# A seven-product step that adds one product onto ScalarE's copy in PSUM, and joins one pair more

## The chip, the cores and the metric

The kernel runs on one core of one Trainium2 chip. A core has TensorE (matrix products, PE in the profile, with its weight loads as PEld), VectorE (DVE), ScalarE (ACT), GpSimd (POOL) and SyncE (SP, which issues DMAs here). Each engine works through its own queue in order; engines wait for each other through semaphores. The metric is the time of one execution on the device in microseconds (us).

## The reference

```python
for t in range(S):                       # attention block: B, H, S, D = 4, 8, 768, 48
    cur = einsum('bhd,bhe->bhde', u * k[t], v[t])
    y[t] = einsum('bhd,bhde->bhe', r[t], state + cur)
    state = w[t][..., None] * state + einsum('bhd,bhe->bhde', k[t], v[t])
x = y.transpose(0, 2, 1, 3).reshape(B * S, H * D)      # 3072 tokens x 384
h = x @ w_in                                           # 384 -> 2048
g = h - tanh(h)
return g @ w_out                                       # 2048 -> 384
```

All arrays are float32. This case is about the product `x @ w_in`.

## The kernel before

The 3072 tokens are handled in eight blocks of 384 (`NB`; a half, `HB`, is 192). While block i passes through the dense part, the attention part of block i + 1 is computed in the gaps. The order of the work on TensorE, VectorE, ScalarE and SyncE is written out by hand: what the Python code emits first is first in its engine's queue. Inside a block the loop runs over f = 0 to 15, one tile of 128 of the 2048 inner columns at a time.

**First product.** An unjoined f calls `first` (L899): three matmuls of 128x384, one for each third of the 384 inputs, accumulated in the PSUM bank `hp`. The profile shows each float32 matmul as two instructions. Two neighbouring f, a pair j = f // 2, can be *joined* instead: their 2x2 split (two column tiles by two token halves) is computed by a scheme with seven products of the kind Strassen's is, each 192 wide, from sums of weights (`s1` to `s5`, `weight_forms`) and sums of tokens (`t1` to `t4`, `token_forms`) that VectorE makes beforehand. `JOINED` names the joined pairs of each block: three in block 2, six in blocks 3 to 6 (pairs 0, 1, 2, 3, 4, 7), seven in block 7; 34 in all. `Twos.begin` (L948) emits, at the even f, the 11 matmuls of the seven products (L961, 22 instructions), a ScalarE copy of the first product into the SBUF tile `joint` (L962), and four VectorE additions (L971), three of 384 columns and one of 192. The additions come back as a list and are put between VectorE's other work by the loop.

The products land in two PSUM tiles of two banks each, `att0` and `att1` (`ps_a.both`, here e0 and e1; "att" in the profile). The attention part uses the same two tiles for its score products (L508), its state update (L589, read by VectorE at L601) and its results (L785), in turn, through `Kept.tile`.

**After the first product.** `slight` (L987 to L991) emits two tanh per f on ScalarE and a square, which ScalarE or VectorE does; `product` (L905) makes g from them on VectorE; `form_g` (L1010) makes sums of g.

**Second product.** `Fewer` does a scheme of 15 products of 128x128 per pair (L1096). Twelve of them go to the banks `acc0` to `acc2`, six per call of `add`, one call per f through `add_due`. The last three ("others") go to a bank of their own: for pairs 0 to 3 at f = 9, for pairs 4 to 7 during the next block, at f = 0 and f = 2 where its pair 0 is joined; in both cases `hp`. ScalarE copies the first half of them out (L1109), VectorE adds the second half to that (`others_summed`, L1124). The banks `acc` are copied out by ScalarE at the start of the next block (L1109).

**Attention steps in a block** (`plan`): in blocks from 3 on, score products at f = 2, preceded by ScalarE's splits (L556); joins of transposed keys on ScalarE at f = 6 to 9 (L566); state update at f = 10; results at f = 12. VectorE's products at f = 0 and 1 are L450 and L457.

`EMPTY` gives each block a number of no-ops, which `apart` puts between TensorE's matmuls.

Of the kernel before, what the change touches and what calls it, by code (L numbers as in the profile page):

```python
# [37 lines left out]
F32 = mybir.dt.float32  # L38
# [13 lines left out]
P = 128  # L52
L = 64
# [83 lines left out]
def kernel(  # L137
# [59 lines left out]
    def draw(names, cols):  # L197
        nc.gpsimd.memset(mask_all[0:L, cols], 1.0)
        for m in names:
# [5 lines left out]
            else:  # L205
# [13 lines left out]
    states = [states0[:, 0:NPAIR * NCH * L].rearrange("d (p c e) -> d p c e", c=NCH, e=L),  # L219
              const.tile([P, NPAIR, NCH, L], F32, name="states1", tag="states1")]  # L220
# [109 lines left out]
    joint = const.tile([P, 6 * HB], F32, name="joint", tag="joint")  # L330
# [3 lines left out]
    class Block:  # L334
# [258 lines left out]
        def update_2(self):  # L593
# [9 lines left out]
            if self.q > 0:  # L603
                step(St[:, :, 0, 0:D], St[:, :, 0, 0:D], tot(0), ALU.mult)
            for c in range(NCH - 1 if self.q == NQ - 1 else NCH):
                dst = St[:, :, c + 1, 0:D] if c + 1 < NCH else states[self.q + 1][:, :, 0, 0:D]
# [304 lines left out]
    class Twos:  # L911
# [15 lines left out]
        def results(self, *tiles):  # L927
            self.to = [t[:, 0:6 * HB].rearrange("p (n t) -> p n t", t=HB) for t in tiles]
# [19 lines left out]
        def begin(self, ps, j):  # L948

            h = self.to[j % len(self.to)]  # L950
            e0, e1 = ps.both[(ps.n + 1) % 2], ps.both[ps.n % 2]
# [4 lines left out]
            for to, *of in ((e0[:, 1, 0:HB], (a11, b11)), (e0[:, 0, 0:HB], (a12, b21), (a13, b31)),  # L956
                            (e0[:, 0, HB:NB], (s2, t2)), (e1[:, 0, 0:HB], (s3, t3)),
                            (e1[:, 0, HB:NB], (s1, t1), (a23, b32)), (e1[:, 1, 0:HB], (s4, b22), (s5, b32)),
                            (e1[:, 1, HB:NB], (a22, t4), (a23, b31))):
                for n, (lhs, rhs) in enumerate(of):  # L960
                    nc.tensor.matmul(to, lhsT=lhs, rhs=rhs, start=n == 0, stop=n + 1 == len(of))  # L961
            nc.scalar.copy(out=h[:, 3], in_=e0[:, 1, 0:HB])  # L962

            def both(t):
                return t.rearrange("p (n t) -> p n t", t=HB)
# [390 lines left out]
    for i, blk in enumerate(blocks):  # L1356
# [10 lines left out]
        for f in range(NF):  # L1367
# [23 lines left out]
            if joined and f == 9:  # L1391
                fewer.others(ps_a, range(4), hp)
# [225 lines left out]
```

## Time and profile before

| | us |
|---|---|
| median of 3 runs | 537.61 (536.73 to 537.94) |
| the profiled execution | 535.64 |
| its span, first to last instruction | 533.9 |
| TensorE busy (matmuls) | 523.9 (98%) |
| VectorE busy | 478.1 (90%) |
| ScalarE busy | 312.4 (59%) |
| granted TensorE clock | 0.999 |

A row of a grouped view has the line, engine, operation, tiles (out<-in), shape and count, then the busy time, the mean duration of one in ns, and the idle time of the engine just before, with what ended it. A row of the timeline has the start, the length, the engine, line and operation, how many instructions it merges, and in brackets the idle time before it and what ended it. A row of the chain of waits has start, length, engine, tile, line and count.

### The profile page before, as it was taken

What the parts mean: (1) busy time and instruction counts of PE and PEld (TensorE: products, weight loads), DVE (VectorE), ACT (ScalarE), POOL (GpSimd) and SP (SyncE); (2) the same over time, 40 slices, a digit from 0 to 9 for tenths busy, and PEclk for the clock granted to TensorE, in tenths of its full rate; (3) what the DMA queues carried; (4) which work ended last, traced back from release to release, by engine and by line L of the source; (5) the groups of instructions that cost most, each with busy time, mean ns of one, the idle gap of its engine ahead of it and who ended that gap; (6) DMA issues with size and microseconds to landing.
All of it is one profiled execution on the core that took longest, in us unless ns stands there. A gap on an engine that the chain in (4) does not pass through costs nothing.

```text
span 533.9 us, 14969 instructions
## 1 busy us (share of the span) xinstructions
PE 523.9 (98%) x6040; PEld 449.2 (84%) x6040; DVE 478.1 (90%) x1011; ACT 312.4 (59%) x729; POOL 9.1 (2%) x57
## 2 busy tenths in 40 slices
PE   7999999999999999999999999999999999999996
PEld 5756665677887879999799998999889997999994
DVE  7999996698889999999999999999999999667874
ACT  4999984665536473655646375375735655454350
POOL 1100000000000000000000000000000000000001
PEclk9999999999999999999999999999999999999999
DMA  8799632352312452035420832145321430200011
GB/s 282 258 406 342 224 120 71 107 132 64 122 26 72 104 143 95 0 89 166 120 58 2 192 119 66 54 66 142 108 88 31 79 116 1 58 1 1 10 36 48
DMA packets 53048, 56.35 MB, mean 106 GB/s; under 512 B 21488, under 2 KB 50928, under 8 KB 52976
## 3 DMA queue, kind: packets, MB, share of 16 engines
q1 hardware_dynamic: 52592, 55.18, 34.7%
q8 instruction: 49, 0.80, 0.6%
q14 instruction: 23, 0.19, 0.1%
q10 hardware_dynamic: 288, 0.10, 0.1%
q0 software_dynamic: 96, 0.07, 0.1%
HBM read 44.73 MB, written 4.72 MB: 93 GB/s over the span
## 4 chain that ended last, share of the span: by engine, by line
PE 83%; DVE 13%; issue 2%; DMA 1%; SPq 0%; DVEq 0%
PE acc L1096 23%; PE att L961 20%; PE hp L899 17%; PE acc L1047 6%; PE hp L1096 5%; PE att L785 3%; DVE g L1010 2%; PE att L508 2%; DVE joint L971 2%; DVE g L905 1%; PE att L589 1%; DVE pre L431 1%; PE acc L1074 1%; PE att L1096 1%; PE att L899 1%
## 5 line engine op out<-in xcount | busy, mean ns | idle before, releaser
L1096 PE MATMUL acc<-forms,g 128*128 128x128 f32 x972 | 135.5, 276 | 0.0
L1096 PEld LDWEIGHTS acc<-forms,g 128*128 128x128 f32 x972 | 124.3, 192 | 3.8
L899 PE MATMUL hp<-xT,w_sb 128*128 128x384 f32 x330 | 116.5, 489 | 0.0
L1010 DVE TENSOR_TENSOR g<-g 128x256 f32<-128x256 f32 x270 | 110.5, 418 | 6.1 <-DVE g L1010 0.5
L899 PEld LDWEIGHTS hp<-xT,w_sb 128*128 128x128 f32 x330 | 59.5, 190 | 33.3
L905 DVE SCALAR_TENSOR_TENSOR g<-h,qa 128x384 f32<-128x384 f32 x112 | 61.7, 551 | 18.1 <-ACT h L991 17.9
L987 ACT ACTIVATE h<-joint 128x384 f32<-128x384 f32 x54 | 27.9, 517 | 77.5 <-DVE joint L971 77.5
L961 PE MATMUL att<-xT,w_sb 128*128 128x192 f32 x340 | 72.0, 326 | 0.0
L987 ACT ACTIVATE h<-hp 128x384 f32<-128x384 f32 x55 | 27.2, 495 | 58.5 <-PE hp L899 58.4
L991 ACT ACTIVATE h<-h 128x384 f32<-128x384 f32 x113 | 58.2, 515 | 0.0
L961 PEld LDWEIGHTS att<-xT,w_sb 128*128 128x128 f32 x340 | 56.4, 190 | 0.0
L971 DVE TENSOR_TENSOR joint<-joint,att 128x384 f32<-128x384 f32 (+1 forms) x108 | 51.6, 499 | 4.9 <-PE att L961 3.0
L1096 PE MATMUL acc<-w_sb,g 128*128 128x128 f32 x324 | 54.5, 277 | 0.0
L1096 PEld LDWEIGHTS acc<-w_sb,g 128*128 128x128 f32 x324 | 45.9, 192 | 4.4
L961 PE MATMUL att<-turned,kept 128*128 128x192 f32 x192 | 36.5, 327 | 0.1
L1132 DVE TENSOR_TENSOR sums<-sums 128x256 f32<-128x256 f32 x84 | 33.3, 410 | 1.4 <-ACT sums L1109 0.9
L1047 PE MATMUL acc<-w_sb,sums 128*128 128x384 f32 x96 | 33.7, 487 | 0.0
L272 ACT ACTIVATE up<-raw 128x768 f16<-128x768 f32 (+1 forms) x32 | 33.0, 1108 | 0.0
L961 PEld LDWEIGHTS att<-turned,kept 128*128 128x128 f32 x192 | 32.0, 190 | 0.4 <-DVE turned L945 0.4
L1096 PE MATMUL hp<-w_sb,g 128*128 128x128 f32 x176 | 29.5, 275 | 0.0
L1047 PEld LDWEIGHTS acc<-w_sb,sums 128*128 128x128 f32 x96 | 18.1, 190 | 12.3
L988 ACT ACTIVATE qa<-joint 128x384 f32<-128x384 f32 x54 | 27.5, 509 | 0.0
(157 smaller groups left out, 795.5 us busy)
## 6 DMA issues: line engine op xcount, KB each, us to landing
raw<-in_weights SPq DMA_DIRECT2D x16, 768.0 KB, 7.4
w<-in_wT SPq DMA_DIRECT2D x7, 780.0 KB, 4.4
k<-in_kT SPq DMA_DIRECT2D x7, 768.0 KB, 4.6
r<-in_rT SPq DMA_DIRECT2D x7, 768.0 KB, 4.5
v_sb<-in_v SPq DMA_DIRECT2D x8, 576.0 KB, 5.1
k<-in_tokens SPq DMA_DIRECT2D x7, 576.0 KB, 4.1
r<-in_tokens SPq DMA_DIRECT2D x7, 576.0 KB, 4.2
out_y<-sums SPq DMA_DIRECT2D x18, 128.0 KB, 1.9
```

The costliest lines, as they stand in the source:

```text
L272: return lambda: nc.scalar.activation(out=to, in_=of, func=AF.Copy, scale=scale, bias=bias)
L899: nc.tensor.matmul(hp, lhsT=w_in_sb[:, f, kc, :], rhs=xT[kc], start=(kc == KC - 1), stop=(kc == 0))
L905: return lambda: nc.vector.scalar_tensor_tensor(out=out, in0=in0, scalar=scalar, in1=in1, op0=op0, op1=ALU.mult)
L961: nc.tensor.matmul(to, lhsT=lhs, rhs=rhs, start=n == 0, stop=n + 1 == len(of))
L971: return [lambda of=of: nc.vector.tensor_tensor(out=of[0], in0=of[1], in1=of[2], op=ALU.add) for of in ((h[:, 0:5:4], twice(h[:, 3]), both ...
L987: made = nc.scalar.activation(out=t, in_=h, func=AF.Tanh, scale=INNER / UPSCALE)
L988: nc.scalar.activation(out=by, in_=h, func=AF.Tanh, scale=OUTER / UPSCALE)
L991: nc.scalar.activation(out=t, in_=t, func=AF.Square, accum_out=top[:, n:n + 1])
L1010: return lambda: nc.vector.tensor_tensor(out=G[:, to:to + 2], in0=two(G, g_at(q, a0), g_at(q, a1)), in1=two(G, g_at(q, b0), g_at(q, b1)), ...
L1047: nc.tensor.matmul(acc, lhsT=g[:, j * P:(j + 1) * P], rhs=w_out_sb[:, f, :], start=(f == self.first), stop=(f == NF - 1))
L1096: nc.tensor.matmul(to, lhsT=G[:, g_at(q, a), :], rhs=rhs, start=start, stop=stop, skip_group_check=True)
L1132: ops.append(lambda op=op, at=at: nc.vector.tensor_tensor(out=at[0], in0=at[1], in1=at[2], op=OPS[op]))
```

## The change

`Twos.begin` is rearranged. The first product goes to e0's bank 1, and ScalarE copies it to the left half of the bank `hp` (before: to SBUF). s3 t3 and s1 t1 (+ its second term) go to e1's bank 0, and ScalarE copies both, 384 columns, to SBUF; (a22, t4) and its second term go to e1's bank 1; s2 t2 is accumulated by TensorE onto the copy in `hp`. Two additions of 384 columns follow on VectorE. The remaining four matmuls (two terms accumulated onto the first product, and s4, s5) are emitted by a new function `end` after those additions; they follow on TensorE's queue directly, and a third addition of 192 columns works in place in PSUM. The tanh of the pair's first half reads e0's bank 1 instead of SBUF.

`hp` is then no longer free for the others: they go to e0's bank 0, for pairs 4 to 7 all at f = 1 (where the block's pair 0 is joined) and for pairs 0 to 3 at f = 9; they are summed out right ahead of pair 1. Pair 5 is joined in blocks 2 to 6 too, which makes 39 joined pairs; the weight forms of pair 5 move from the set made late for block 7 to a set made in block 2. The order of the two `att` tiles is set anew at the score products and at the state update (`ps.n = 0`). The states lose their padding (64 to 48 columns), `joint` shrinks from six to three halves, and the no-ops are counted anew.

```diff
-BESIDE = (0, 1, 2, 3, 4, 7)
-EMPTY = (159, 0, 92, 0, 16, 0, 40, 0)
-JOINED = {2: (1, 4, 7), 3: BESIDE, 4: BESIDE, 5: BESIDE, 6: BESIDE, 7: TWOS}
-PAIRS = range(0, 1), range(1, 2), range(2, 3), range(3, 5), range(7, 8)
-LEFT = range(5, 7)
+BESIDE = (0, 1, 2, 3, 4, 5, 7)
+EMPTY = (159, 0, 72, 0, 0, 150, 10, 0)
+JOINED = {2: (1, 4, 5, 7), 3: BESIDE, 4: BESIDE, 5: BESIDE, 6: BESIDE, 7: TWOS}
+PAIRS = range(0, 1), range(1, 2), range(2, 3), range(3, 6), range(7, 8)
+LEFT = range(6, 7)
...
+            if name in ("earlier", "update"):
+                ps.n = 0
...
-            h = self.to[j % len(self.to)]
-            e0, e1 = ps.both[(ps.n + 1) % 2], ps.both[ps.n % 2]
+            to, (e0, e1) = self.to[j % len(self.to)], ps.both
...
-            for to, *of in ((e0[:, 1, 0:HB], (a11, b11)), (e0[:, 0, 0:HB], (a12, b21), (a13, b31)),
-                            (e0[:, 0, HB:NB], (s2, t2)), (e1[:, 0, 0:HB], (s3, t3)),
-                            (e1[:, 0, HB:NB], (s1, t1), (a23, b32)), (e1[:, 1, 0:HB], (s4, b22), (s5, b32)),
-                            (e1[:, 1, HB:NB], (a22, t4), (a23, b31))):
-                for n, (lhs, rhs) in enumerate(of):
-                    nc.tensor.matmul(to, lhsT=lhs, rhs=rhs, start=n == 0, stop=n + 1 == len(of))
-            nc.scalar.copy(out=h[:, 3], in_=e0[:, 1, 0:HB])
+            c11, c12 = (e0[:, 1, n * HB:(n + 1) * HB] for n in range(2))
+            sixth = hp[:, 0:HB]
+
+            def products(*groups):
+                for to, start, *of in groups:
+                    for n, (lhs, rhs) in enumerate(of):
+                        nc.tensor.matmul(to, lhsT=lhs, rhs=rhs, start=start and n == 0, stop=n + 1 == len(of),
+                                         skip_group_check=True)
...
-            return [lambda of=of: nc.vector.tensor_tensor(out=of[0], in0=of[1], in1=of[2], op=ALU.add)
-                    for of in ((h[:, 0:5:4], twice(h[:, 3]), both(e0[:, 0, 0:NB])),
-                               (h[:, 5:3:-1], twice(h[:, 4]), both(e1[:, 0, 0:NB])),
-                               (h[:, 1], h[:, 4], e1[:, 1, 0:HB]),
-                               (h[:, 2:4], twice(h[:, 5]), e1[:, 1::-1, HB:NB]))]
+            products((c11, True, (a11, b11)))
+            nc.scalar.copy(out=sixth, in_=c11)
+            products((e1[:, 0, 0:HB], True, (s3, t3)), (e1[:, 0, HB:NB], True, (s1, t1), (a23, b32)))
+            nc.scalar.copy(out=to[:, 2::-2], in_=e1[:, 0, 0:NB].rearrange("p (n t) -> p n t", t=HB))
+            products((e1[:, 1, HB:NB], True, (a22, t4), (a23, b31)), (sixth, False, (s2, t2)))
+
+            def end():
+                products((c11, False, (a12, b21), (a13, b31)), (c12, False, (s4, b22), (s5, b32)))
+                return [adding(c12, to[:, 0], c12)]
+
+            self.end = end
+            self.h = [e0[:, 1, 0:NB], to[:, 1:3].rearrange("p n t -> p (n t)")]
+            return [adding(to[:, 2::-2], to[:, 2::-2], twice(sixth)),
+                    adding(to[:, 1:3], twice(to[:, 2]), e1[:, 1::-1, HB:NB])]
...
             if joined and f == 9:
-                fewer.others(ps_a, range(4), hp)
+                fewer.others(ps_a, range(4), ps_a.both[0][:, 0])
+            if joined and f == 1 and summed:
+                summed[0].others(ps_a, (4, 5, 6, 7), ps_a.both[0][:, 0])
...
-            if f == 3 and summed and 0 in JOINED.get(i, ()):
-                spare.append(summed[0].others_summed)
...
-            elif outs and later:
-                ops = between(rest, carried) + outs[:1] + formed + outs[1:] + spare
-                carried = []
             elif outs:
-                ops = (between(rest, carried) + outs[:1] + formed + spare[:-1] + outs[1:2] + spare[-1:] + outs[2:])
-                carried = []
+                early_spare, spare = ([], spare) if later else (spare[:-1], spare[-1:])
+                run(between(rest, carried) + outs[:1] + formed + early_spare + outs[1:])
+                ops, carried = twos.end() + spare, []
             elif joined and later:
-                ops, behind = behind + between(forming, spare) + rest + formed, []
+                ops = (between(forming + rest + formed, behind) + spare if len(behind) > 2 else
+                       behind + between(forming, spare) + rest + formed)
+                behind = []
...
-                if f in (0, 2) and summed and 0 in JOINED[i]:
-                    summed[0].others(ps_a, (4,) if not f else (5, 6, 7), hp)
...
+            if joined and f == 1 and summed:
+                behind.append(summed[0].others_summed)
```

More of the change, by code (lines that the diff above doesn't have):

```diff
@@ L329 @@
     turned = const.tile([P, 2 * NB], F32, name="turned", tag="turned")
-    joint = const.tile([P, 6 * HB], F32, name="joint", tag="joint")
+    joint = const.tile([P, 3 * HB], F32, name="joint", tag="joint")
     empty = []
@@ L927, in results @@
         def results(self, *tiles):
-            self.to = [t[:, 0:6 * HB].rearrange("p (n t) -> p n t", t=HB) for t in tiles]
+            self.to = [t[:, 0:3 * HB].rearrange("p (n t) -> p n t", t=HB) for t in tiles]
         def weight_forms(self, n, which):
@@ L1324 @@
     twos = Twos()
-    for pairs, at in zip(PAIRS, (0, 1, 2, 3, 5)):
+    for pairs, at in zip(PAIRS, (0, 1, 2, 3, 6)):
         twos.form(pairs, [kept[:, (x * len(BESIDE) + at) * P:(x * len(BESIDE) + at + len(pairs)) * P]
@@ L1484 @@
             if i == 1 and f == 6:
[L1485 removed]
+                nc.gpsimd.memset(states[0][:, :, 0], 0.0)
             if not i and "update" in phases.get(f, ()):
@@ L1556 @@
             make_identity(nc, unit[0])
-            for st in states:
-                nc.vector.memset(st[:, :, :, D:], 0.0)
             for blk in [Block(b, q) for b in range(B) for q in range(NQ)]:
```

16 lines of the change are left out of this document (7 added, 9 removed).

## The prediction

> **What bounds the kernel now.** I read the page's busy shares and chain first, then a table by stage over one block of tokens, then the chain of waits by line inside that block.
>
> ```profile
> span 533.9 us, 14969 instructions
> ...
> PE 523.9 (98%) x6040; PEld 449.2 (84%) x6040; DVE 478.1 (90%) x1011; ACT 312.4 (59%) x729; POOL 9.1 (2%) x57
> ...
> PE 83%; DVE 13%; issue 2%; DMA 1%; SPq 0%; DVEq 0%
> ```
> ```profile
> 277.60:340.30 62.70, 62.70 (x767) 58.61 (x767) 60.36 (x129) 35.75 (x92) 0.32 (x4) 1.00 0.36 92
> ```
> ```profile
> 301.18 3.58 PE att L961 x22
> 304.76 2.68 PE acc L1096 x24
> ...
> 318.39 1.43 PE att L589 x80
> 319.81 1.53 PE acc L1096 x12
> 321.35 1.94 PE hp L899 x6
> 323.29 1.34 PE acc L1096 x12
> ```
>
> The second fence is block 4 (columns: window, its length, busy PE, PEld, DVE, ACT, POOL, granted clock, DMA share, GB/s). TensorE is busy for 62.70 of 62.70 us and VectorE for 60.36. So whatever makes TensorE wait inside a block is added to the time, and whatever VectorE sheds is worth only what TensorE waited for it, which here is nearly nothing. A joined pair costs TensorE 3.58 us (22 matmuls, 0.163 each); an unjoined pair costs two runs of 1.94, so 3.88; six products of the second stage cost 1.34, the 12 matmuls of one call.
>
> **What it removes and adds.** Pair 5 becomes joined in blocks 2 to 6: TensorE gains 3.88 - 3.58 = 0.30 us five times, 1.5 us. Joined pairs go from 34 to 39. Each loses one 384-wide addition and gains a 384-wide ScalarE copy out of PSUM:
>
> ```profile
> L971 DVE TENSOR_TENSOR joint<-joint,att 128x384 f32<-128x384 f32 x81 | 44.3, 547 | 4.0 <-PE att L961 3.0 <-ACT joint L962 1.0
> L971 DVE TENSOR_TENSOR joint<-joint,att 128x192 f32<-128x192 f32 x27 | 9.6, 354 | 0.9
> L757 ACT COPY xT<-att 128x384 f32<-128x384 f32 x22 | 9.2, 496 | 0.0
> L1010 DVE TENSOR_TENSOR g<-g 128x256 f32<-128x256 f32 x270 | 110.5, 418 | 6.1 <-DVE g L1010 0.5 <-PE acc L1096 0.3
> L905 DVE SCALAR_TENSOR_TENSOR g<-h,qa 128x384 f32<-128x384 f32 x112 | 61.7, 551 | 18.1 <-ACT h L991 17.9
> ```
>
> VectorE sheds 34 x 0.55 = 18.6 us and takes 5 x (2 x 0.55 + 0.35) = 7.2 us for the new pairs, so it ends about 11 us lighter; ScalarE takes 39 x 0.50 = 19 us more on 312. The addition that writes to PSUM has no row; the same size in SBUF is 0.35 and I take that. All of this lies beside TensorE's work, so I cost it at nothing on the path. The forms of pair 5's weights move between two sets whose total stays; the narrower state tiles change strides only; the no-ops are issued between matmuls of at least 0.11 us. These too I cost at nothing (0.3 us either way).
>
> **The wait that is new.** Before, no TensorE instruction inside a run of joined products waits for ScalarE. After, two do: s2 t2 adds onto ScalarE's copy in hp, and (a22, t4) writes bank 1 of tile e1 after ScalarE was told to copy bank 0 of it. Whether the second is a wait depends on how the program's waits are set, by bank or by tile. The run at 334.04 answers it for reads:
>
> ```profile
> 334.04 1.14 PE L961 MATMUL att<-xT,w_sb 128*128 128x192 f32 x6
> ...
> 335.02 1.14 PE L961 MATMUL att<-turned,kept 128*128 128x192 f32 x6
> ...
> 335.54 0.32 ACT L962 COPY joint<-att 128x192 f32<-128x192 f32 x1 [1.26 <-PE att L961]
> ...
> 338.84 0.52 ACT L987 ACTIVATE h<-joint 128x384 f32<-128x384 f32 x1 [2.98 <-DVE joint L971]
> ...
> 339.27 0.51 ACT L988 ACTIVATE qa<-joint 128x384 f32<-128x384 f32 x1
> ...
> 340.19 0.51 ACT L987 ACTIVATE h<-joint 128x384 f32<-128x384 f32 x1
> ```
>
> The copy reads the first product alone, which is two matmuls and lands at 334.04 + 0.163 + 0.33 = 334.53. ScalarE stood idle for 1.26 us and still began at 335.54. That is when the eighth matmul lands (334.04 + 7 x 0.163 + 0.33 = 335.51), the last into tile e0, in its other bank. So a read waits for the whole two-bank tile. For writes no stall in the trace isolates the question, but the program's list of waits does: the matmul that opens the results (L785) waits for the state addition (L601) that reads the other bank of its tile, though neither its own bank nor its operands need that one. I take it that the rule is the tile.
>
> Then (a22, t4) waits in every joined pair. The eighth matmul lands at 1.47 us from the start of the run, the copy begins at 1.50 (as above), takes 0.50 (L757), and TensorE starts 0.05 us behind its releaser, as here, where the merged additions end at 228.70 + 1.40 = 230.10:
>
> ```profile
> 228.70 1.40 DVE L971 TENSOR_TENSOR joint<-joint,att 128x384 f32<-128x384 f32 x3
> ...
> 230.15 0.64 PE L508 MATMUL att<-pre,post 48*64 48x64 f32 x28 [0.72 <-DVE joint L971]
> ```
>
> That is 2.05, or 2.15 with a weight load that nothing hides, where it would have issued at 8 x 0.163 = 1.30: 0.75 to 0.85 us. I take 0.80, so **39 x 0.80 = 31 us**. Bounds: 29 and 33; nothing at all if waits go by bank.
>
> **What the wait drags behind it.** After, the tanh of a pair's first half hangs on a chain through all engines: the run is 3.58 + 0.80 = 4.38 long, VectorE's last addition follows at about 4.85 to 5.20, both tanh are over at 6.2 (0.94 from 338.84 to 339.78), and ScalarE is free after two halves of 1.35 each (338.84 to 340.19), at 7.95. Against that stand, in a full block, with these rows:
>
> ```profile
> 287.34 2.94 ACT L556 COPY w<-post 128x768 uint16<-128x768 uint16 x3
> ...
> 287.94 0.95 DVE L450 TENSOR_TENSOR pre<-r,pre 128x768 f32<-128x768 f32 x1
> ...
> 290.18 1.09 ACT L1109 ACTIVATE sums<-acc 128x512 f32<-128x512 f32 x2
> ...
> 291.58 1.81 PE L508 MATMUL att<-pre,post 48*64 48x64 f32 x96
> ```
> ```profile
> 309.67 0.75 ACT L566 COPY ks<-ks 128x512 uint16<-128x512 uint16 x1
> ...
> 310.29 0.30 ACT L962 COPY joint<-att 128x192 f32<-128x192 f32 x1
> ```
> ```profile
> 317.36 2.02 ACT L566 COPY ks<-post 128x512 uint16<-128x512 uint16 x3
> ...
> 321.77 0.35 DVE L601 TENSOR_TENSOR states<-states,whole 128x192 f32<-128x192 f32 x1
> ...
> 326.51 0.36 DVE L601 TENSOR_TENSOR states<-states,whole 128x192 f32<-128x192 f32 x1
> ...
> 327.83 1.56 PE L785 MATMUL att<-pre,states 48*48 48x64 f32 x96
> ```
>
> - The fourth-column products ("others") at f = 1 and f = 9 now write tile e0, which tanh still reads: TensorE is there at 4.38 + 1.34 = 5.72 and waits to 6.25: 0.5 us, twice.
> - Pair 1's first product waits for VectorE to sum those products out of e0. VectorE, from 5.20: one product of 0.95, three of 0.95, three forms and another at 0.42, one of 0.55, and the sum of 0.55, to 11.8. TensorE, from 6.25: 24 matmuls of 0.112 (2.7) and 1.34, to 10.3. 1.5 us.
> - The second score product at f = 2 writes e0 and so waits for pair 1's tanh, behind ScalarE's three splits (2.0 + 2.94) and the two copies of 1.09 that need TensorE's 5.9: to 7.0, then 0.94. TensorE is there at 5.72 + 0.9: 1.35 us. Before, the moved products covered this.
> - Pair 4: two joins of 0.75 hold ScalarE to 9.45, and TensorE begins at 4.38 + 2.68 = 7.06; the copies of 0.32 and 0.50 end 3.2 into the run, not 2.0: 1.2 us. (At 310.29 the copy is this late already, 3.0 us into the run at 307.3, and nothing waits.)
> - Pair 5, by the same count with the 0.75 and 2.02 joins and the copy of the others' half: 1.5 us.
> - The results (L785) wait for the states: VectorE takes 5.1 us (321.77 to 326.87), TensorE's cover shrinks from 8.0 us (319.82 to 327.83) to 1.34 + 1.94 + 1.34 = 4.6, and VectorE starts behind pair 5's additions: 1.5 us.
>
> That is 8.05 us in each of blocks 3 to 6, some 3.5 in block 2 (the others at f = 9, pair 5, the results) and 1.0 in block 7 (the others twice): 37 us. Each stands on a queue position that I derived and shrinks when VectorE, 0.55 us lighter per pair, is ahead; I take six tenths, 22 us. Ends: -1 (none, and the small stall at 230.15 gone) and 44.
>
> **Sum.** Against the profiled execution's 535.64 us (1.7 us around its span; the median of the runs is 2.0 above it): 535.6 - 1.5 + 31 + 22 = 587, so **589 us** as a median; I say 590.
>
> **Rivals.**
> 1. *Waits go by bank*, and only the read's wait was late. For it: the change keeps each engine in a bank of its own. Against it: the copy at 335.54, held by the other bank. Without the 31 us, the score product (1.35), the results (1.5) and pair 4 keep their waits; pair 4's is then s2 t2 behind the copy in hp: ScalarE is free at 9.45 - 0.80 = 8.65, the run begins at 3.58 + 2.68 = 6.26, so the copy ends 2.7 into it and is needed at 12 x 0.163 = 1.96: 0.75 us. That is 3.6 x 4 + 2.2 (block 2) - 1.5 = 15: 553 us. The Trainium skill states the rule that this rival needs, in "PSUM — Partial Sum Buffer", "Summary: rules for kernel authors": a read beside running matmuls should aim at another bank, and semaphores guard by bank; by it nothing would have to wait at the ninth matmul, and the trace of before shows this program waiting for more than that.
> 2. *Faster.* By bank, and VectorE, lighter by 0.55 per pair, brings tanh so far forward that no copy is late: TensorE keeps the 1.5 us and the stall of 0.72 at 230.15, and the time is about 535.5. It decides from where ScalarE is free 1.2 us into each run. For it: ScalarE is 59% busy. Against it: 310.29.
> 3. *The change gives nothing.* The 1.5 us is lost again to one or two waits per block: 537.6.
>
> **How the numbers follow.** The forecast, waits by tile, 0.86; rival 1, 0.04; rival 2, 0.07; rival 3, 0.03. The forecast's own range runs from 537.6 + 29 - 1.5 - 1 = 564 to 537.6 + 33 + 44 - 1.5 = 613; I give **560 to 616**, which leaves out the rivals and a little more. A measurement of this kernel tells about 0.2% (1.1 us) from nothing. Faster 0.07, within 0.2% 0.03, slower 0.90.
>
> **What would show it.** In the profile after, the run of 22 matmuls should be cut in two or three pieces, with TensorE idle about 0.8 us in front of the ninth matmul, released by the copy of the two products, 39 times; the waits view should hold a row of TensorE on that copy of some 30 us and more. TensorE's busy share should fall to about 90%, and VectorE's busy time to about 467 us. The forecast falls if the ninth matmul follows the eighth after 0.16 us; then rivals 1 and 2 are parted by the score product at f = 2 and the results. The second sum falls if the ninth waits and the grams, the others and L785 do not: then it is about 567.

## The result: 595.4 us after, 537.5 before

| | before | after |
|---|---|---|
| median of the runs | 537.49 (536.73 to 537.94) | 595.35 (594.42 to 597.78) |
| profiled execution | 535.64 | 594.77 |
| its span | 533.9 | 593.0 |

The ratio is 1.1085, 95% interval 1.1048 to 1.1122: slower by 58 us. The forecast was 590, range 560 to 616.

From the page of the changed kernel, its span, busy times and the chain by engine:

```profile
span 593.0 us, 15237 instructions
...
PE 538.7 (91%) x6090; PEld 457.2 (77%) x6090; DVE 469.5 (79%) x992; ACT 329.5 (56%) x773; POOL 9.1 (2%) x57
...
PE 62%; DVE 17%; ACT 13%; issue 4%; DMA 2%; SPq 1%; PEld 0%; PEldq 0%; DVEq 0%; ACTq 0%
```

TensorE was 98% busy and is 91% busy; on the chain its share falls from 83% to 62%, and ScalarE, which was not on it, has 13%. VectorE ended 8.6 us lighter (478.1 to 469.5) and ScalarE 17.1 heavier, as the change intends. None of that is the 58 us. It is TensorE's waits, here by what it waited for (us in total, times, longest):

```profile
PE att L965 <- ACT joint L977: 27.7, 32, 1.8
PE att L508 <- ACT qa L1000: 4.3, 4, 1.1
PE att L1108 <- ACT qa L1000: 3.4, 5, 0.9
PE att L965 <- ACT pre L977: 2.6, 4, 0.9
PE att L965 <- DVE sums L1136: 2.3, 4, 0.7
...
PE att L965 <- ACT w L977: 1.7, 3, 0.6
...
PE att L785 <- DVE states L601: 0.5, 1, 0.5
```

The first, fourth and sixth row are one wait, on the copy of e1's bank 0 (L977; the tile it goes to is `joint`, or `pre` and `w` in the last block): 32 + 4 + 3 = 39 times, once in each joined pair. The grouped view of the instructions has the same 39 as one group of 78 matmuls (two for each) with 32.0 us of idle ahead:

```profile
L965 PE MATMUL att<-turned,w_sb 128*128 128x192 f32 x78 | 23.1, 378 | 32.0 <-ACT joint L977 27.7 <-ACT pre L977 2.6 <-ACT w L977 1.7
...
L977 ACT COPY joint<-att 128x384 f32<-128x384 f32 x32 | 15.3, 478 | 13.6 <-PE att L965 13.5
L972 DVE TENSOR_TENSOR att<-joint,att 128x192 f32<-128x192 f32 x32 | 11.4, 356 | 0.0
```

These rows understate the loss, because the profile models the ends of matmuls and part of a stall stands as busy time: counted from start to start of the matmuls, as below, the 39 waits come to 38.3 us.

The new copy takes 0.48 us (0.50 was assumed), the addition into PSUM 0.36 (0.35). The prices of single instructions were right.

The table by stage for block 4, whose length before was 62.70 us:

```profile
297.13:370.23 73.10, 64.84 (x777) 59.91 (x776) 59.04 (x126) 39.01 (x101) 0.32 (x4) 1.00 0.31 79
```

It is 10.4 us longer at the same granted clock (1.00), and TensorE, once busy all through, idles 8.3 us of it. In its timeline (start, length, engine, line, tile, count, idle before and its releaser) each loss can be read:

```profile
298.11 0.49 PE L965 MATMUL att<-xT,w_sb 128*128 128x192 f32 x2
298.69 0.48 ACT L977 COPY joint<-att 128x384 f32<-128x384 f32 x1 [0.41 <-PE att L965]
...
299.22 0.59 PE L965 MATMUL att<-turned,w_sb 128*128 128x192 f32 x2 [0.62 <-ACT joint L977]
...
302.71 0.39 PE L1108 MATMUL acc<-forms,g 128*128 128x128 f32 x2
...
303.55 0.49 PE L1108 MATMUL att<-w_sb,g 128*128 128x128 f32 x2 [0.45 <-ACT qa L1000]
...
306.78 1.06 PE L1108 MATMUL acc<-forms,g 128*128 128x128 f32 x8
...
308.52 0.59 PE L965 MATMUL att<-xT,w_sb 128*128 128x192 f32 x2 [0.68 <-DVE sums L1136]
```
```profile
316.53 0.93 PE L508 MATMUL att<-pre,post 48*64 48x64 f32 x48 [1.08 <-ACT qa L1000]
```
```profile
344.37 1.99 ACT L566 COPY ks<-post 128x512 uint16<-128x512 uint16 x3
...
344.77 0.49 PE L965 MATMUL att<-xT,w_sb 128*128 128x192 f32 x2
...
346.51 0.47 ACT L977 COPY joint<-att 128x384 f32<-128x384 f32 x1
347.03 0.59 PE L965 MATMUL att<-turned,w_sb 128*128 128x192 f32 x2 [1.78 <-ACT joint L977]
```

The ninth matmul (as the profile counts them, two for each product; it is the first of (a22, t4)) should follow the seventh by 2 x 0.163; at pair 0 it follows by 299.22 - 298.11 = 1.11, so the stall is 0.78. At pair 5 the same wait is 347.03 - 344.77 - 0.33 = 1.93, because ScalarE's joins (344.37, 1.99 us) stand ahead of both copies. Between these lie the others at f = 1 behind tanh (303.55 - 302.71 - 0.22 = 0.62), pair 1's first product behind VectorE's sum (308.52 - 306.78 - 8 x 0.112 = 0.84), and the second score product behind pair 1's tanh (1.08 of idle).

From pair 0 to the next block's pair 0, blocks 3 to 6 are 10.38, 10.43, 10.59 and 10.95 us longer than before. Block 2, from its first joined pair on, is 8.05 longer, block 7 is 7.67 longer, and 1.07 lie ahead of any joined pair: 59.1 in all, the difference of the two spans.

### The profile page after: what moved, and what is told of

It is laid out like the page before. It is cut to its first block, busy times and chain, and to the rows that moved or that the text cites. A ratio compares the mean times of both kernels' runs of the same rounds, so it can differ in the third digit from the quotient of the medians.

```text
span 593.0 us, 15237 instructions
## 1 busy us (share of the span) xinstructions
PE 538.7 (91%) x6090; PEld 457.2 (77%) x6090; DVE 469.5 (79%) x992; ACT 329.5 (56%) x773; POOL 9.1 (2%) x57
## 4 chain that ended last, share of the span: by engine, by line
PE 62%; DVE 17%; ACT 13%; issue 4%; DMA 2%; SPq 1%; PEld 0%; PEldq 0%; DVEq 0%; ACTq 0%
PE att L965 15%; PE acc L1108 15%; PE hp L901 13%; PE acc L1059 5%; PE att L1108 5%; DVE g L1022 3%; PE att L785 3%; DVE joint L972 2%; ACT h L999 2%; ACT joint L977 2%; ACT qa L1000 2%; ACT ks L566 2%; PE hp L965 2%; ACT h L1003 2%; DMA w<-in_wT 2%
## 5 line engine op out<-in xcount | busy, mean ns | idle before, releaser
L901 PE MATMUL hp<-xT,w_sb 128*128 128x384 f32 x270 | 95.5, 490 | 0.0
L965 PE MATMUL att<-xT,w_sb 128*128 128x192 f32 x390 | 89.6, 328 | 3.8 <-DVE sums L1136 2.3
L999 ACT ACTIVATE h<-att 128x384 f32<-128x384 f32 x42 | 20.7, 493 | 108.7 <-DVE att L972 108.7
L901 PEld LDWEIGHTS hp<-xT,w_sb 128*128 128x128 f32 x270 | 48.8, 190 | 28.1 <-ACT qa L1000 0.4
L972 DVE TENSOR_TENSOR joint<-joint,hp 128x384 f32<-128x384 f32 x32 | 17.7, 552 | 44.2 <-PE hp L965 44.2
L965 PE MATMUL att<-turned,w_sb 128*128 128x192 f32 x78 | 23.1, 378 | 32.0 <-ACT joint L977 27.7
L965 PEld LDWEIGHTS att<-turned,w_sb 128*128 128x128 f32 x78 | 11.6, 188 | 43.5 <-ACT joint L977 37.1
L1108 PE MATMUL att<-w_sb,g 128*128 128x128 f32 x216 | 36.6, 281 | 3.7 <-ACT qa L1000 3.4
L1108 PEld LDWEIGHTS att<-w_sb,g 128*128 128x128 f32 x216 | 29.9, 191 | 6.6 <-ACT qa L1000 5.8
L965 PE MATMUL att<-xT,kept 128*128 128x192 f32 x152 | 30.9, 326 | 0.0
```

The costliest lines, as they stand in the source:

```text
L901: nc.tensor.matmul(hp, lhsT=w_in_sb[:, f, kc, :], rhs=xT[kc], start=(kc == KC - 1), stop=(kc == 0))
L965: nc.tensor.matmul(to, lhsT=lhs, rhs=rhs, start=start and n == 0, stop=n + 1 == len(of), skip_group_check=True)
L972: return lambda: nc.vector.tensor_tensor(out=out, in0=in0, in1=in1, op=ALU.add)
L999: made = nc.scalar.activation(out=t, in_=h, func=AF.Tanh, scale=INNER / UPSCALE)
L1108: nc.tensor.matmul(to, lhsT=G[:, g_at(q, a), :], rhs=rhs, start=start, stop=stop, skip_group_check=True)
```

## The experiments

The time of the kernel before, taken beside them, was 537.2 to 538.1.

### Is it the tile? The kernel before with one line moved

```diff
                 for n, (lhs, rhs) in enumerate(of):
                     nc.tensor.matmul(to, lhsT=lhs, rhs=rhs, start=n == 0, stop=n + 1 == len(of))
-            nc.scalar.copy(out=h[:, 3], in_=e0[:, 1, 0:HB])
+                if of[0][0] is a11:
+                    nc.scalar.copy(out=h[:, 3], in_=e0[:, 1, 0:HB])
```

> The kernel before, with one line moved: ScalarE is told to copy the first product right behind its two matmuls, and not behind all 22; the nine others follow. If a write waits for a read of the other bank of its tile (my theory, by tile), the third matmul, into e0's bank 0, waits for that copy of bank 1: the product lands 0.49 us into the run, the copy of 192 columns takes 0.32, so TensorE goes on at 0.92 to 1.0 in place of 0.33, 0.6 to 0.7 us in each of 34 pairs, 20 to 24 us, and later tanh may add up to 10: 558 to 571 us, with a row of TensorE's L961 waiting for ScalarE. If waits go by bank, nothing in the run waits, the copy only comes earlier: 537.5, within 1 us.

Measured: 583.14 us (581.8 to 585.2), ratio 1.0858 (1.0820 to 1.0895). By bank nothing would have changed; so the wait by tile is there, in a kernel that has nothing else of the change. But it is twice the size expected. The largest row of its waits, and two places in its timeline:

```profile
PE att L961 <- ACT joint L963: 27.6, 27, 2.3
```
```profile
308.37 0.49 PE L961 MATMUL att<-xT,w_sb 128*128 128x192 f32 x2
...
308.95 0.32 ACT L963 COPY joint<-att 128x192 f32<-128x192 f32 x1 [1.75 <-PE att L961]
...
309.32 0.92 PE L961 MATMUL att<-xT,w_sb 128*128 128x192 f32 x4 [0.46 <-ACT joint L963]
```
```profile
324.73 0.75 ACT L566 COPY ks<-ks 128x512 uint16<-128x512 uint16 x1
...
325.35 0.30 ACT L963 COPY joint<-att 128x192 f32<-128x192 f32 x1
325.70 0.92 PE L961 MATMUL att<-xT,w_sb 128*128 128x192 f32 x4 [2.28 <-ACT joint L963]
```

Where ScalarE is idle (308.95, it had waited 1.75 us for the product) the stall is 309.32 - 308.37 - 0.33 = 0.62, the 0.6 to 0.7 expected. Where ScalarE still has the last pair's tanh and a join to do, the copy starts at 325.35 and TensorE waits 2.3 us. Ahead of the 27 pairs outside the last block alone TensorE idles 27.6 us. What I left out was ScalarE's queue: the copy is short, but it stands behind tanh of the pair before. A part is TensorE's clock: behind each of the four waits of 2.28 us the granted clock fell to 0.50 for 3.41 us, which is up to 4 x 3.41 x 0.50 = 6.8 us of the time (an estimate, as if TensorE were the bound all through these stretches). Without it the run would still lie above the range expected.

### The same order in the changed kernel, turned round

```diff
-            nc.scalar.copy(out=to[:, 2::-2], in_=e1[:, 0, 0:NB].rearrange("p (n t) -> p n t", t=HB))
-            products((e1[:, 1, HB:NB], True, (a22, t4), (a23, b31)), (sixth, False, (s2, t2)))
+            products((e1[:, 1, HB:NB], True, (a22, t4), (a23, b31)))
+            nc.scalar.copy(out=to[:, 2::-2], in_=e1[:, 0, 0:NB].rearrange("p (n t) -> p n t", t=HB))
+            products((sixth, False, (s2, t2)))
```

> The changed kernel, with ScalarE's copy of e1's bank 0 emitted behind the (a22, t4) products in place of ahead of them; the matmuls keep their order. By tile: the copy now waits for the tenth matmul instead of the seventh, and the ninth waits for nothing; 39 x 0.75 = 29 us go, and the copy ends 0.5 us later into the run, which VectorE's additions can bear: 564 to 569 us, and no row of L965 waiting for the copy of 384 columns. If the wait of the ninth has another cause than the copy's place in the program (the bank, or two engines at the same memory), it stays: 590 to 595. If the stall only moves to what hangs on the later copy (VectorE, tanh, and TensorE behind them): 575 to 585.

Measured: 574.16 us (571.55 to 575.16), ratio 1.0678 (1.0639 to 1.0718): 21.2 less than the changed kernel. The wait on the copy of 384 columns is gone, all 32.0 us of it, but other waits have grown:

```profile
PE att L1109 <- ACT qa L1001: 8.6, 8, 2.0
PE att L508 <- ACT qa L1001: 5.5, 4, 1.4
PE hp L965 <- ACT hp L975: 4.7, 9, 0.7
```

The others wait 5.2 us more for tanh than before the edit (8.6 against 3.4), the score product 1.2 more, and s2 t2 now waits 4.7 for the copy in hp, which had been covered. So the ninth matmul's wait has its cause in the place of the copy, as forecast.

In idle time these rows come to -32.0 + 5.2 + 1.2 + 4.7 = -20.9, close to the 21.2 measured, but they leave out TensorE's clock. In the profiled execution the granted clock fell to 0.50 five times, for 3.41 us each, behind waits of TensorE of 0.9 to 2.0 us. One of the five (the clock is the third number from the end):

```profile
300.24:303.65 3.41, 3.41 (x18) 3.41 (x17) 3.31 (x7) 0.68 (x3) 0.00 (x0) 0.50 0.00 0
```

In the changed kernel's profiled execution this happens only at its very end. In such a stretch the matmuls of 192 columns start 0.32 us apart in place of 0.163. The five stretches are worth up to 5 x 3.41 x 0.50 = 8.5 us. Without them the run would take about 566 us (an estimate), inside the 564 to 569 expected. So the shortfall of 7.8 us against the 29 expected is no larger than what the clock can have taken. The stall that went was itself larger than priced (38.3 us start to start), so the next waits and the clock both have room in the account, and their shares stay open.

### The same moment, another tile

```diff
-            products((e1[:, 1, HB:NB], True, (a22, t4), (a23, b31)), (sixth, False, (s2, t2)))
+            products((e0[:, 0, HB:NB], True, (a22, t4), (a23, b31)), (sixth, False, (s2, t2)))
...
-                    adding(to[:, 1:3], twice(to[:, 2]), e1[:, 1::-1, HB:NB])]
+                    adding(to[:, 1], to[:, 2], e0[:, 0, HB:NB]),
+                    adding(to[:, 2], to[:, 2], e1[:, 0, HB:NB])]
...
-                run(between(rest, carried) + outs[:1] + formed + early_spare + outs[1:])
-                ops, carried = twos.end() + spare, []
+                run(between(rest, carried) + outs[:1] + formed + early_spare)
+                ops, carried = twos.end() + outs[1:] + spare, []
```

> The changed kernel, with (a22, t4) and its second term written to bank 0 of tile e0 in place of bank 1 of e1, so that the copy of e1's bank 0 runs beside a write into the other tile at the same moment as before. The addition that read both banks of e1 becomes two of 192 columns, and the last four matmuls are emitted ahead of them (they would else wait for VectorE's read of e0). VectorE gets 39 x 0.16 = 6 us more. By tile: the wait of 0.75 goes from 39 pairs: 562 to 570 us. If TensorE cannot write while ScalarE reads this memory, whatever the tile, the time stays at 590 to 600, with the ninth matmul as late as it was.

Measured: 582.48 us (582.19 to 583.58), ratio 1.0845 (1.0818 to 1.0873). The total lies between the two expectations; the timeline at pair 1 and the waits say why:

```profile
307.03 0.30 ACT L975 COPY hp<-att 128x192 f32<-128x192 f32 x1 [1.46 <-PE att L965]
307.48 0.49 PE L965 MATMUL att<-xT,w_sb 128*128 128x192 f32 x2
307.80 0.49 PE L965 MATMUL att<-turned,w_sb 128*128 128x192 f32 x2
308.06 0.48 ACT L977 COPY joint<-att 128x384 f32<-128x384 f32 x1 [0.73 <-PE att L965]
```
```profile
PE att L965 <- ACT hp L975: 14.1, 13, 1.4
PE att L1109 <- ACT qa L1001: 10.2, 11, 1.7
```

At 307.80 the ninth matmul starts 0.32 us behind the seventh, with no wait, and ScalarE's copy of e1 (308.06 to 308.54) runs beside the next ones. So here TensorE writes one tile in PSUM while ScalarE reads another. Where the write now waits it waits for the other copy, L975, which reads the first product in the *other bank of tile e0*, the tile that it was moved to (13 times, where that copy is late). The wait follows the tile, not the bank. (No run here lets a matmul write one bank of a tile while ScalarE reads the other, so whether the chip could do that is not shown. The Trainium skill's page "PSUM — Partial Sum Buffer", in its "Summary: rules for kernel authors", puts the guarding of PSUM by semaphores at the bank; the waits of this program are coarser, as these runs show.)

### The others in the other tile

```diff
-                fewer.others(ps_a, range(4), ps_a.both[0][:, 0])
+                fewer.others(ps_a, range(4), ps_a.both[1][:, 0])
...
-                summed[0].others(ps_a, (4, 5, 6, 7), ps_a.both[0][:, 0])
+                summed[0].others(ps_a, (4, 5, 6, 7), ps_a.both[1][:, 0])
```

> The changed kernel, with the others at f = 1 and f = 9 written to e1's bank 0 in place of e0's bank 0, which the tanh of the pair's first half still reads. By tile they then wait for VectorE's second addition alone, which is over: the stalls ahead of them (0.2 to 1.1 us each, about 5.4 us in all) go, and pair 1's first product no longer waits for VectorE's sum of the others; the third matmul of that pair does, 0.33 us later, so up to 1.5 us more: 588 to 590 us. If that time is only handed to the next wait (the second score product, behind tanh on ScalarE's queue), less than 2 us is gained: 593 to 595.

Measured: 592.64 us (591.54 to 594.88), ratio 1.1045 (1.1010 to 1.1079), 2.7 less than the changed kernel, between the two (the intervals of the two ratios overlap, so this is hardly more than the noise). The wait of the others for tanh (3.4 us) is gone. The profiled execution has one stretch of 3.41 us at clock 0.50, up to 1.7 us. TensorE's wait for VectorE's sum has grown from 2.3 to 5.0 us, because what it wins arrives early at the next place:

```profile
PE att L965 <- DVE sums L1136: 5.0, 4, 1.5
```

### Pair 5, taken out of the changed kernel and put into the old one

Out: `BESIDE`, `JOINED`, `PAIRS` and `LEFT` as before. In: those four as after, with

```diff
-                    for of in ((h[:, 0:5:4], twice(h[:, 3]), both(e0[:, 0, 0:NB])),
-                               (h[:, 5:3:-1], twice(h[:, 4]), both(e1[:, 0, 0:NB])),
-                               (h[:, 1], h[:, 4], e1[:, 1, 0:HB]),
-                               (h[:, 2:4], twice(h[:, 5]), e1[:, 1::-1, HB:NB]))]
+                    for of in ((h[:, 0:2], twice(h[:, 3]), both(e0[:, 0, 0:NB])),
+                               (h[:, 3:0:-2], twice(h[:, 1]), both(e1[:, 0, 0:NB])),
+                               (h[:, 1], h[:, 1], e1[:, 1, 0:HB]),
+                               (h[:, 2:4], twice(h[:, 3]), e1[:, 1::-1, HB:NB]))]
```

> The changed kernel, with pair 5 unjoined in blocks 2 to 6 as before (34 joined pairs). In the trace of the changed kernel pair 5's ninth matmul waits 1.94 us in every full block, the longest of all. If pair 5 costs what stands there: 3.58 + 1.94 = 5.52 us go and 3.88 come, five times, 8.2 us: about 587 us. If that wait is only handed to it by work that would hold another instruction up in its absence (the joins on ScalarE, the states on VectorE), it goes to the results or the update: 592 to 595 us.

> The kernel before, with pair 5 joined too and nothing else of the change: its own order of matmuls, copy and additions. To make room for the weight forms, the states are narrowed as in the change, and the additions keep their sums in four halves of the tile joint instead of six. By my third step: 5 x 0.30 = 1.5 us less, 536.0 (535.4 to 536.6). If pair 5's four additions, about 2.0 us of VectorE in place of none, hold up the states and the results behind them, nothing or a loss: 537.5 to 541.

Out: 582.70 us (582.11 to 583.05), ratio 1.0842 (1.0821 to 1.0864), 12.7 less than the changed kernel, more than the 8.2 that pair 5's own stall and its 0.30 come to. Blocks 3 to 6 of the profiled execution are 2.0, 2.1, 1.7 and 0.7 us shorter than in the changed kernel, about the 1.64 a block of that sum; the surplus is in block 2, 5.45 shorter. In: 557.72 us (555.17 to 558.92), ratio 1.0383 (1.0363 to 1.0404). So joining pair 5 in the old order does not gain 1.5 us, the kernel becomes 20 longer. A row of its waits, the second half of block 4 in the table by stage, and about the same stretch of the kernel before:

```profile
PE acc L1096 <- DVE g L1010: 12.0, 9, 2.6
```
```profile
318.00:349.00 31.00, 27.99 (x432) 25.20 (x431) 29.86 (x65) 16.88 (x44) 0.32 (x4) 1.00 0.29 82
```
```profile
306.00:336.00 30.00, 30.00 (x440) 26.19 (x440) 28.78 (x63) 19.18 (x49) 0.32 (x4) 1.00 0.32 93
```

Before, TensorE is busy for 30.00 of 30.00 us in that stretch and VectorE for 28.78. With pair 5, VectorE is busy for 29.86 of 31.00 and TensorE for 27.99: VectorE has become the bound there, and the second products wait for its sums of g. Pair 5 brings VectorE 3 x 0.55 + 0.35 = 2.0 us and there were 1.2 to spare. That gives the cause but not the whole size: block 4 is 3.3 us longer, and blocks 3, 5 and 6 are 1.5, 3.8 and 2.9 longer. Block 2, where VectorE also makes the weight forms, is 6.8 longer; up to 3.4 of that is the clock, 0.50 for 6.83 us behind a wait of 2.6 us for sums of g. Two gaps of 2.1 us together in blocks 5 and 6, ahead of the results, have no releaser in the profile. So of the 20 us some 14 are left for VectorE's load, 12.0 of which stand as waits for sums of g. What the dropped addition is good for may be this room for a seventh pair; that the room comes from it alone was not tried. (The additions also work in place here; their mean stayed at 0.55 us, and block 7, with seven pairs in both kernels, takes 69.1 us against 68.9.)

### Mending what the trace shows, one cause after the other

First the second and fourth experiment together:

> The changed kernel with two of the edits together: the copy of e1's bank 0 behind the (a22, t4) products, and the others in e1's bank 0. Alone they took 21.2 and 2.7 us. With the first edit alone the trace shows TensorE losing 24.5 us in L1109's runs, ahead of the others (2.15 us each at f = 1) where the changed kernel lost 14.8: what the ninth matmul no longer waits for, the others wait for, behind tanh. If that is so, the two together take more than the sum of both, 562 to 568 us; if VectorE's sum of the others takes the place of tanh, the sum: 571 to 573.

Measured: 565.05 us (563.95 to 565.50), ratio 1.0511 (1.0488 to 1.0533). That is 30.3 less than the changed kernel, where the two alone took 21.2 and 2.7. But this does not show that the two waits stood one behind the other. From the pages, first the run with the first edit alone, then this one:

```profile
PE 538.7 (94%) x6090; PEld 466.3 (81%) x6090; DVE 468.9 (82%) x992; ACT 329.2 (58%) x773; POOL 9.1 (2%) x57
```
```profile
PE 529.6 (94%) x6090; PEld 457.4 (81%) x6090; DVE 468.3 (83%) x992; ACT 329.4 (58%) x773; POOL 9.1 (2%) x57
```

The spans are 572.2 and 563.1, so TensorE idles 33.5 us in both: the wait of the others for tanh (8.6) is gone, but the waits for VectorE's sum (0.9 to 5.2) and for its additions ahead of the others (0 to 4.2) have taken its place. The whole 9.1 us are busy time of the same 6090 matmuls, and this run has no stretch at clock 0.50 before its end, where the first edit alone had five, worth up to 8.5. What the others' new place gained here is TensorE's clock, not idle time; the mean granted clock of the four runs each is 0.980 to 0.991 and 0.994 to 1.000. Then ScalarE's order:

```diff
-                if near and f and i > 2:
-                    for name in ("split 2 0", "split 2 1", "split 0 01"):
-                        later.phase(ps_a, name)
+                for name in joins:
+                    behind += later.phase(ps_a, name)
+                joins = []
...
-                add_due(now)
                 g, made, square, later_ops = slight(twos.h[0], now, i, f)
+                add_due(now)
+                if near and f and i > 2:
+                    for name in ("split 2 0", "split 2 1", "split 0 01"):
+                        later.phase(ps_a, name)
...
-                        behind += later.phase(ps_a, name)
+                        if name.startswith("join") and f in (7, 9) and (f + 1) // 2 in JOINED.get(i, ()):
+                            joins.append(name)
+                        else:
+                            behind += later.phase(ps_a, name)
```

> The same two edits, and ScalarE's order around them: the tanh of a pair's first half ahead of the copies out of acc, ScalarE's three splits at f = 2 behind that tanh and not ahead of it, and the joins of f = 7 and f = 9 behind the next pair's two copies and not ahead of them. My theory puts the second score product's stall (1.3 to 1.6 us in each of four blocks) and the late copy into hp at pairs 4 and 5 (0.44 and 0.89 us in the run with the ninth matmul freed, five times) on this order: 13 us less than the same without it, so 550 to 558 us. If the splits and joins only push the next tanh back by as much, and TensorE waits for that, the time is that of the two edits within 3 us.

Measured: 556.45 us (555.61 to 557.16), ratio 1.0350 (1.0329 to 1.0372). 8.6 of the 13 us came. TensorE's waits in this run:

```profile
PE att L965 <- DVE sums L1137: 5.2, 4, 1.5
PE hp L965 <- ACT hp L975: 3.8, 4, 1.0
...
PE att L1109 <- DVE joint L972: 3.6, 4, 0.9
```

The score product's wait for tanh (5.5 us) is no longer among them, and pairs 4 and 5 do not wait. But the splits, put behind tanh, make the copy of pair 2 late (the second row, a wait that was not there), so part of the gain was handed on. The next run gives each of these three rows its own remedy:

```diff
-                fewer.others(ps_a, range(4), ps_a.both[1][:, 0])
+                fewer.others(ps_a, range(4), hp)
...
-                summed[0].others(ps_a, (4, 5, 6, 7), ps_a.both[1][:, 0])
+                summed[0].others(ps_a, (4, 5, 6, 7), hp)
...
+            if joined and f == 1 and summed:
+                spare.insert(len(spare) - 1, summed[0].others_summed)
...
+                if later and i > 2:
+                    joins += {2: ["split 2 0", "split 2 1"], 4: ["split 0 01"]}.get(f, [])
```

> As the run with ScalarE's order mended, with two edits more. The others go to the bank hp as in the kernel before (all four at f = 1), which the first addition of a pair frees early, and VectorE's sum of them stands one place further ahead in f = 1. Two of ScalarE's splits stand behind the copies of pair 1 and the third behind those of pair 2, where ScalarE idles before tanh. In the trace of the run with ScalarE's order mended, what is left of stalls in a full block is 1.07 us ahead of the others, 1.63 ahead of pair 1's third matmul (behind VectorE's sum), and 1.11 ahead of pair 2's s2 t2 (behind a late copy to hp): 14.6 us in blocks 3 to 6. If each is due to the tile or the place in the queue that I name: 556.5 - 14.6 = 542 us (540 to 545). If the copy to hp at pair 1 then waits for the sum and TensorE for it: 546 to 552.

Measured: 541.59 us (539.97 to 542.79), ratio 1.0087 (1.0069 to 1.0105), as expected. And with `JOINED[2]` as in the kernel before:

> The same without pair 5 in block 2 (38 joined pairs), where the additions for it meet VectorE's forms of weights: in the trace of the run with ScalarE's order mended TensorE loses 1.68 us at the end of block 2 waiting for sums of g and 1.09 and 0.75 us around it. If VectorE's load there is the cause: 2.5 to 3.2 us less than with pair 5, 538 to 541 us, beside 538 for the kernel before. If not, the same time or 0.3 us more.

Measured: 537.81 us (536.31 to 538.72), ratio 1.0009 (0.9997 to 1.0022), 3.8 less, a little more than expected. Blocks 4 and 5 of this run, from pair 0 to the next block's pair 0:

```profile
279.14:341.59 62.45, 62.44 (x776) 59.94 (x774) 58.58 (x126) 39.00 (x100) 0.32 (x4) 1.00 0.34 91
341.59:404.77 63.18, 63.07 (x776) 60.26 (x774) 58.26 (x125) 38.98 (x100) 0.32 (x4) 1.00 0.36 91
```

TensorE is busy throughout again, and block 4 takes 62.45 us where it took 62.67. But block 5 takes 63.18 where it took 62.35, and block 3, which had the stall at 230.15 before, takes 1.1 less; blocks 3 to 6 together take 250.7 against 251.1. So the gain of pair 5, forecast at 0.30 a block, cannot be told from the rest. Two runs more looked for it:

```diff
+                if f != 2 or not 2 < i < blocks_n - 1:
+                    add_due(now)
                 g, made, square, later_ops = slight(twos.h[0], now, i, f)
```

> As the run without pair 5 in block 2, with the copies out of acc ahead of tanh again wherever no splits follow (all f but f = 2 of blocks 3 to 6). In the trace of the run without this TensorE loses 0.43 us twice behind those copies, at 167 and 482 us. If the order is the cause: 0.9 us less, 537.0, beside 537.4 for the kernel before, which is not to be told from it. It also settles what the repaired change is worth at most: TensorE gains 4 x 0.30 = 1.2 us, and I expect no more than that, 536 to 538.

```diff
-EMPTY = (159, 0, 72, 0, 0, 150, 10, 0)
+EMPTY = (159, 0, 92, 0, 16, 0, 40, 0)
```

> The same with the numbers of no-ops of the kernel before. I priced them at nothing (0.3 us either way): within 0.3 us of the run beside it. If the 150 no-ops in block 5 hold TensorE up, 1 to 3 us less; if they cover a stall elsewhere, as much more.

The first: 537.92 us (536.83 to 539.25), ratio 1.0017 (1.0004 to 1.0030); no gain on the run before it. The two stalls named are gone, but two first products now wait for tanh instead, 1.2 us together. The second: 539.88 us (538.46 to 540.63), ratio 1.0051 (1.0032 to 1.0071), 2.0 more than the first, where I had expected no difference. A row of its waits:

```profile
PE att L785 <- issue: 2.4, 2, 1.4
```

"issue" is time in which TensorE waits for nothing that the profile shows. With the changed kernel's counts of no-ops these two gaps, 2.4 us together, are not there. One of them, 1.0, lies in block 5, where the changed kernel has 150 no-ops, and costs nothing in the end: the block takes 63.15 us with the no-ops and 63.19 with the gap. The other, 1.4, lies in block 6, which takes 62.45 and 63.68. What the gaps are was not tried.

No version beat the kernel before; the mended one equals it within 0.2%.

## Why the prediction was right, and where its steps were off

**The wait by tile: right in cause and size.** 39 waits on the copy, as forecast; 0.73 to 0.79 us in 28 of them, against 0.80 (0.75 to 0.85), and 1.05 to 1.94 in the other 11, where the copy came later still. Moving the write behind the copy's place removed it, moving the read ahead in the old kernel made it, and moving the write to another tile moved the wait to that tile's reader. The rival "by bank" (553 us) falls with any of the three; "faster" and "gives nothing" fell with the time itself.

**The waits behind it: the mechanism right, the terms off in both directions.** For a full block I listed 8.05 us and took six tenths, 4.83. What block 4 shows, next to the full terms:

| | forecast | measured |
|---|---|---|
| others at f = 1 | 0.5 | 0.62 |
| others at f = 9 | 0.5 | 0.22 |
| pair 1's first product | 1.5 | 0.84 |
| second score product | 1.35 | 1.08 of idle, 1.29 start to start |
| pair 4, beyond the 0.78 | 1.2 | 0.52 |
| pair 5, beyond the 0.78 | 1.5 | 1.15 |
| results (L785) | 1.5 | 0 |

The 1.29 is 316.53 less the first score product's start at 314.52, less 48 matmuls of 0.015. The rows of f = 9 and pair 4 are starts of neighbouring matmuls less their usual distance, as above:

```profile
334.10 0.49 PE L965 MATMUL att<-xT,w_sb 128*128 128x192 f32 x2
...
335.73 0.59 PE L965 MATMUL att<-turned,w_sb 128*128 128x192 f32 x2 [1.15 <-ACT joint L977]
...
339.23 0.39 PE L1108 MATMUL acc<-forms,g 128*128 128x128 f32 x2
...
339.67 0.49 PE L1108 MATMUL att<-w_sb,g 128*128 128x128 f32 x2
```

They come to 4.6, with the 1.29 for the score product, against 4.83. That six tenths fitted a full block is luck in part: it was one guess for all terms, and they were mis-sized one by one: the results' wait, 1.5, does not exist (one wait of 0.5 in the whole run, behind the states), since VectorE is ahead by then; the waits for tanh and for the copies were right in kind. The total came out 5 us above the 590 mainly because of the rest. By the forecast's terms a full block is 7 x 0.80 + 4.83 - 0.30 = 10.1 us longer, and blocks 3 to 6 are 10.38 to 10.95 longer, 42.4 together. For block 2 the terms give 4 x 0.80 + 0.6 x 3.5 - 0.3 = 5.0, and it is 8.0 longer; for block 7 they give 7 x 0.80 + 0.6 x 1.0 = 6.2, and it is 7.7. Block 2 was put too low: leaving pair 5 out of it took 3.8 us away even from the mended kernel, and I had given all its waits behind the copy 0.6 x 3.5 = 2.1.

**Pair 5 at +1.5 us: wrong as priced.** That step counted TensorE's 0.30 a block and let VectorE's 2.0 us lie "beside TensorE's work". In the old order they do not fit, and the kernel was 20 us longer, some 14 of them without the clock and the gaps. In the mended order, where six pairs have shed 0.55 each, they fit in blocks 3 to 6, but no gain of 0.30 a block can be told. Inside the changed kernel pair 5 cost 12.7 us: 6.5 in blocks 3 to 6, as the pair with the longest wait, and 5.45 in block 2 (profiled executions). The error was to price VectorE's load as a net sum over the whole change (11 us lighter), which is right for the change but does not give a price of this part.

**The no-ops at 0.3 us: wrong.** Their numbers are worth 2.0 us in the mended kernel (1.2 between the two profiled executions). In the comparison of before and after this did not show, since the change counts them anew.

**What would show it.** The forecast busy share of TensorE, 90%, was 91%; the wait on the copy, "30 us and more", was 32.0; the stall ahead of the ninth matmul came 39 times; VectorE's 467 was 469.5. The ninth matmul followed the eighth late in every joined pair, so the condition under which the forecast falls did not occur.

## What to carry to other kernels

Where a copy and a matmul share a PSUM tile, look at which of the two is emitted first, not only at the banks: in this program a write waits for an earlier read of any bank of its tile, and emitting the matmul ahead of the copy took 21 us away at no cost in work, although TensorE's clock gave some of the gain back. Putting a short ScalarE instruction into the middle of a TensorE run prices TensorE by ScalarE's queue, not by the instruction's own 0.3 or 0.5 us. When two runs differ, compare TensorE's idle time, its busy time and the granted clock before putting the difference down to a wait: here the clock was worth up to 8.5 us. Of a saving on an engine that is 96% busy ask what it makes room for: where TensorE is busy throughout, the addition saved here shortens nothing by itself, and a pair that is joined without such savings made the kernel longer, not shorter.

## What was not expected of the hardware

The granted TensorE clock fell to 0.50 behind some waits of TensorE: for 3.41 us four times with the copy moved early in the old kernel (each behind a wait of 2.28 us) and five times with the copy put behind the ninth matmul, and for 6.83 us once with pair 5 in the old kernel (behind 2.59 us, with 1.30 more inside). Such a wait then costs up to 3.41 x 0.50 = 1.7 us more than its own length (an estimate). The length of the wait alone does not decide it: the changed kernel has five waits of 1.77 or 1.78 us with no fall behind them, and a stretch in the run with the others in e1 follows waits of 1.1 and 0.6. What decides was not tried.

Two gaps of 2.4 us together at L785, which the profile puts down to no releaser, come and go with the number of no-ops between earlier matmuls (539.88 against 537.92 us). Such gaps stand at L785 also in the two runs with pair 5 taken out and put in (1.3 and 2.1 us).

And one negative: TensorE's matmuls into one tile run at their usual distance of 0.163 us while ScalarE copies out of another (307.80 in the run with the ninth matmul moved to the other tile), so between these two tiles nothing but the program's own waits kept them apart.
